# Attention followed by a two-layer MLP: scores in groups of three chunks between whole groups of MLP products, and two shared PSUM banks

## The chip, the core and the metric

The kernel runs on one core of a Trainium2 chip. The metric is the device time of one execution in microseconds (us), and the median over several runs is quoted. Every profile is one execution of its own.

The engines are named as in the profile. PE is TensorE, which multiplies matrices (PEld is its weight load, which overlaps the products). ACT is ScalarE, DVE is VectorE, POOL is GpSimd, and SP is SyncE, which here only issues transfers. SPq is SyncE's queue. PSUM is the memory in which TensorE leaves its results[...].

## The reference

```python
scores = (1.0 / np.sqrt(64)) * np.matmul(q, k.transpose(0, 1, 3, 2))   # q, k, v: (8, 12, 448, 64)
scores = scores - np.max(scores, axis=-1, keepdims=True)
attn = np.exp(scores)
attn = attn / (np.sum(attn, axis=-1, keepdims=True) + 1e-09)
x = np.matmul(attn, v)                                                 # (8, 12, 448, 64)
x = x.transpose(0, 2, 1, 3).reshape(3584, 768)
h = x @ w_in                                                           # (768, 2048)
g = np.maximum(0.01 * h, h)
out = g @ w_out                                                        # (2048, 768), float32
```

The kernel leaves out the subtraction of the maximum. It multiplies in bf16 and accumulates in float32.

## The kernel before

**Units.** A unit `u` is a pair of heads of one batch. There are 8 batches with 6 pairs each, so 48 units (`NU`), and `HP` is 6. For every unit, q, k and v are loaded by SyncE (`load`, L91), cast to bf16 by GpSimd (`cast`, L104), and q and k are turned so that the head dimension lies on partitions (`qkT`). The first 12 units (`NPE`) are turned by TensorE into PSUM (`transposes`, L164) and copied out by VectorE (L173). Later units are turned by a transposing transfer on SyncE's queue (`dma_transposes`, L160).

**Scores.** A unit has four chunks of 112 keys. `scores(u, c)` (L177) makes two products, one for each head of the pair. Each uses 64 rows of the array and has 448 columns. The two results lie in the two banks of one score slot (pool `ps_s`). `expo(u, c)` (L189) lets ScalarE take the exponential of both at once (L191) and write `e`, which frees the slot.

**pv.** `pv(u, j)` (L193) makes 16 small products for one head of the pair, each with 65 columns, the last of which is the sum of the exponentials. VectorE takes the reciprocal (L207) and multiplies (L208). The result `x` is turned into `xT` by `x_transposes` (L212): through TensorE and a VectorE copy for units below 9, and by a transposing transfer for the later ones.

**MLP.** `mlp(i)` (L236) works on 384 or 512 tokens in turn, four batches of each, the first with 384. It has 16 groups of six products for the first layer (L243, called w_in below), each group evacuated by ScalarE (L248). Then it has 6 or 8 groups of 16 products with 384 columns for the second layer (L260, called w_out below), each evacuated by VectorE (L265). A finished row block of `o` is stored by SyncE (`store`, L225). `mlp` is a generator: it hands back control after every single product.

**Order.** The order is written out by hand, so every engine runs its instructions in the order of the program. `slots(u)` (L306) gives eight steps for a unit: scores of two chunks in step 0, their exponentials in steps 0 and 1, `pv` of the unit before in steps 2 and 6, transposes in steps 1 and 3, the scores of the other two chunks in step 4. The first six units run alone (L362). From then on, 60 steps are spread over the products of MLP batch 0 and 48 steps over each of batches 1 to 6. The steps fall between single products, wherever the count of columns says so (L370 to L376). Batch 7 has no attention beside it.

**PSUM.** There are two score slots of two banks each (`ps_s`), one bank for transposes (`ps_tr`), one bank for pv (`ps_pv`), and two for MLP products (`ps_mm`), L58 to L61. A product that starts a new result in a slot waits for the last reader of the old one.

**Weights.** `load_w` issues eight transfers from GpSimd's queue, one early and seven in units 2 to 5.

Of the kernel before, what the change touches and what calls it, by code (L numbers as in the profile page):

```python
# [16 lines left out]
def kernel(  # L17
# [9 lines left out]
    nc = tc.nc  # L27
# [27 lines left out]
    h_pool = ctx.enter_context(tc.tile_pool(name="h", bufs=2))  # L55
    o_pool = ctx.enter_context(tc.tile_pool(name="o", bufs=3))

    ps_s = ctx.enter_context(tc.tile_pool(name="ps_s", bufs=2, space=PSUM))  # L58
    ps_tr = ctx.enter_context(tc.tile_pool(name="ps_tr", bufs=1, space=PSUM))
    ps_pv = ctx.enter_context(tc.tile_pool(name="ps_pv", bufs=1, space=PSUM))  # L60
    ps_mm = ctx.enter_context(tc.tile_pool(name="ps_mm", bufs=2, space=PSUM))  # L61


    NV = 5
# [67 lines left out]

    def warm_up(n):
        for _ in range(n):
            ps = ps_mm.tile([P, 512], F32, name="mm")
            nc.tensor.matmul(ps, warm[:, :P], warm, start=True, stop=True)  # L136

    warm_up(9)
# [21 lines left out]
    def dma_transposes(u):  # L160
        if NPE <= u < NU:
            turn(qkT[u % NQ][:, :QL], qk_sb[u].rearrange("p i so h d -> p (i so h d)"))

    def transposes(u):  # L164
        if u >= min(NPE, NU):
            return
        tr = ps_tr.tile([P, 2, S], BF16, name="tr")
        for i in range(2):
            for so in range(NSC):
                nc.tensor.transpose(  # L170
                    tr[:, i, ts(so, SC)], qk_sb[u][:, i, so], ident[:SC, :SC]
                )
        nc.vector.tensor_copy(qkT[u % NQ][:, :QL], tr.rearrange("p i s -> p (i s)"))  # L173
# [19 lines left out]
    def pv(u, j):  # L193

        e, vt = e_sb[u % NE], v_sb[u % NV]
        ps = ps_pv.tile([P, NSC, D + 1], F32, name="pv")
        for qc in range(NSC):
            for c in range(NSC):
                at = (j * NSC + c) * S + qc * SC
                nc.tensor.matmul(  # L200
                    ps[:, qc, :], e[:, at:at + P], vt[:, j, c, :],
                    start=(c == 0), stop=(c == NSC - 1),
                )
        if j == 0:
            x_t[u] = x_pool.tile([SC, NSC, 2, D], BF16, name="x")
        rec = r_pool.tile([SC, NSC, 1], F32, name="rec")
        nc.vector.reciprocal(rec, ps[:SC, :, D:])  # L207
        nc.vector.tensor_mul(  # L208
            x_t[u][:, :, j, :], ps[:SC, :, :D], rec.to_broadcast([SC, NSC, D])
        )  # L210

    def x_transposes(u):  # L212
        b, hp = divmod(u, HP)
        at = b * S % NX
        dst = xT[:, hp, at:at + S]
        if u >= NPE - 3:
            turn(dst, x_t.pop(u).rearrange("p so h d -> p (so h d)"))
            return
        tr = ps_tr.tile([P, 2, S], BF16, name="tr")
        for so in range(NSC):  # L220
            nc.tensor.transpose(tr[:, 0, ts(so, SC)], x_t[u][:, so], ident[:SC, :SC])  # L221
        nc.vector.tensor_copy(dst, tr[:, 0, :])  # L222


    def store(o, t0):  # L225

        done = 0
        while done < P:
# [4 lines left out]
            nc.sync.dma_start(out=dst[so, p:p + n], in_=o[done:done + n, :])  # L233
            done += n

    def mlp(i):  # L236
        n = cuts[i + 1] - cuts[i]
        at = cuts[i] % NX
        h = h_pool.tile([P, MD, 4 * P], BF16, name="h")
        for m in range(MD):  # L240
            ps = ps_mm.tile([P, 4 * P], F32, name="mm")
            for kk in range(KD):
                nc.tensor.matmul(  # L243
                    ps[:, :n], w_in_sb[:, kk, ts(m, P)], xT[:, kk, at:at + n],
                    start=(kk == 0), stop=(kk == KD - 1),
                )
                if kk == KD - 1:
                    nc.scalar.activation(h[:, m, :n], ps[:, :n], AX.Prelu, alpha=0.01)  # L248
                yield n

        todo = [(c, w) for c in range(n // P) for w in range(2)]
        if i == 0:
            todo.sort(key=lambda cw: cw[1])
        o = {}
        for c, w in todo:
            if c not in o:
                o[c] = o_pool.tile([P, DM], F32, name="o")
            ps = ps_mm.tile([P, 4 * P], F32, name="mm")
            for m in range(MD):
                nc.tensor.matmul(  # L260
                    ps[:, :NW], h[:, m, ts(c, P)], w_out_sb[:, m, ts(w, NW)],
                    start=(m == 0), stop=(m == MD - 1),
                )
                if m == MD - 1:
                    nc.vector.tensor_copy(o[c][:, ts(w, NW)], ps[:, :NW])  # L265
                    if w == 1:
                        store(o.pop(c), cuts[i] + c * P)
                yield NW


    def turning_slots(u):


        def s0():
            pv(u - 1, 0)
            x_transposes(u - 2)

        def s1():
            pv(u - 1, 1)
            transposes(u)  # L280

        def s2():
            x_transposes(u - 1)

        def s3():
            scores(u, 0)
            scores(u, 1)
            expo(u, 0)
            load(u + 5)

        def s4():
            expo(u, 1)
            transposes(u + 1)

        def s5():
            scores(u, 2)
            scores(u, 3)
            expo(u, 2)
            cast(u + 3)

        def s6():
            expo(u, 3)

        return [s0, s1, s2, s3, s4, s5, s6, lambda: None]

    def slots(u):  # L306

        on = u < NU

        def s0():  # L310
            if on:
                scores(u, 0)
                scores(u, 1)
                expo(u, 0)
            if u == 0:
                warm_up(4)

        def s1():
            if on:
                expo(u, 1)  # L320
            if 2 <= u <= NU + 1 and u - 2 not in (HP - 2, HP - 1):
                x_transposes(u - 2)
            dma_transposes(u + 2)

        def s2():
            if 1 <= u <= NU:
                pv(u - 1, 0)

        def s3():
            load(u + 5)  # L330
            load_w({2: 1, 3: 2, 4: 2, 5: 2}.get(u, 0))
            if u + 1 < NU and u + 1 != HP:
                transposes(u + 1)

        def s4():
            if on:
                scores(u, 2)
                scores(u, 3)
                expo(u, 2)

        def s5():
            if on:
                expo(u, 3)
            cast(u + 3)

        def s6():
            if 1 <= u <= NU:
                pv(u - 1, 1)

        def s7():  # L350
            pass

        return [s0, s1, s2, s3, s4, s5, s6, s7]

    steps = [s for u in range(NU + 2) for s in (turning_slots if u == HP else slots)(u)]

    begin = [8 * (HP * (i + 1) + 1) + 7 for i in range(B)]
    begin[0] = 8 * HP + 3
    assert begin[B - 1] == 8 * (NU + 1) + 7
    transposes(0)  # L360
    warm_up(2)
    for s in steps[:begin[0]]:  # L362
        s()
    for i in range(B):
        work = steps[begin[i]:begin[i + 1]] if i + 1 < B else []
        n = cuts[i + 1] - cuts[i]
        total = MD * KD * n + n // P * MD * DM
        used = 0
        atoms = mlp(i)
        for j, s in enumerate(work):  # L370
            s()
            while used < total * (j + 1) // len(work):
                step = next(atoms, None)
                if step is None:
                    break
                used += step  # L376
        for _ in atoms:
            pass


# [28 lines left out]
```

## Time and profile before

| | us |
|---|---|
| median of 7 runs | 427.86 |
| lowest and highest run | 426.55 and 429.44 |
| time of the profiled execution | 428.95 |
| its span, first to last instruction | 427.2 |

| group of the profile | count | busy, us | mean of one, ns |
|---|---|---|---|
| L191 exponential, ACT | 192 | 167.9 | 915 |
| L243 w_in products, PE | 768 | 163.3 | 355 |
| L260 w_out products, PE | 896 | 160.7 | 326 |
| L200 pv products, PE | 1536 | 65.1 | 194 |
| L182 score products, PE | 384 | 54.7 | 357 |
| L248 first-layer evacuation, ACT | 128 | 69.8 | 545 |
| L265 second-layer evacuation, DVE | 56 | 31.2 | 557 |
| L208 and L207 after pv, DVE | 96 each | 40.7 and 17.5 | 424 and 182 |

How to read it: products on TensorE are pipelined, so the mean duration of one is longer than its share of the engine. The distance between two starts is what a product costs. The busy time of a group is the time in which at least one of its instructions ran.

TensorE's clock is granted in full except in the stretch from 30 to 40 us, where the mean is 0.66. The 16 transfer engines are saturated over the first 80 us (207 to 287 GB/s in stretches of 10 us), since the weights come in beside q, k and v.

### The profile page before, as it was taken

Reading aid. Unit: us, or ns where it says so; the run is one execution under the profiler, and the core shown is the slowest. Engines: PE = TensorE matmul, PEld = TensorE weight load, DVE = VectorE, ACT = ScalarE, POOL = GpSimd, SP = SyncE. Lnnn points to the kernel's source line nnn. Section 1 sums busy time; section 2 is a strip of 40 time slices with the busy share of each in tenths; the row PEclk is TensorE's granted clock in tenths of the full one; section 3 lists DMA queues with packets and bytes.
Section 4 is the critical chain, followed back from the end, with each engine's and each line's share of the span. In section 5 each row is a group of like instructions: output and inputs, shape, how many; then the busy total and the mean of one; then the engine's idle time right before and its main releaser. Section 6 shows DMA issues by size and latency. Waiting matters only on the chain.

```text
span 427.2 us, 8997 instructions
## 1 busy us (share of the span) xinstructions
PE 414.1 (97%) x3731; PEld 226.9 (53%) x3731; DVE 100.2 (23%) x271; ACT 229.8 (54%) x322; POOL 92.1 (22%) x168
## 2 busy tenths in 40 slices
PE   7879999999999999999999999999999999999995
PEld 2554665544555555544455555554455555654563
DVE  1542333221132212221122212221123211320021
ACT  4866775567634676457643476456753477314300
POOL 4494332331111222211311131221112100000000
PEclk9997999999999999999999999999999999999999
DMA  8999999984555966675374977686445440230022
GB/s 207 255 245 246 249 250 215 267 221 109 111 143 160 209 130 167 180 184 137 97 146 126 185 181 136 183 193 153 128 99 142 112 90 13 59 85 2 0 75 74
DMA packets 98505, 63.66 MB, mean 149 GB/s; under 512 B 55456, under 2 KB 94880, under 8 KB 98464
## 3 DMA queue, kind: packets, MB, share of 16 engines
q1 hardware_dynamic: 90928, 56.56, 55.5%
q0 software_dynamic: 7296, 6.29, 9.2%
q8 instruction: 29, 0.48, 0.5%
q10 hardware_dynamic: 240, 0.23, 0.2%
q14 instruction: 12, 0.10, 0.1%
HBM read 45.61 MB, written 11.01 MB: 133 GB/s over the span
## 4 chain that ended last, share of the span: by engine, by line
PE 94%; ACT 2%; DMA 1%; issue 1%; POOL 1%; DVE 1%; SPq 0%; ACTq 0%
PE mm L243 35%; PE mm L260 35%; PE pv L200 11%; PE sc L182 10%; ACT e L191 2%; PE tr L170 1%; DMA fv<-in_v_dram 1%; PE tr L221 0%; POOL w_in_sb L124 0%; DVE x L208 0%; DVE qkT L173 0%; POOL qkb L109 0%; POOL v L111 0%; POOL qkb L110 0%; DVE o L265 0%
## 5 line engine op out<-in xcount | busy, mean ns | idle before, releaser
L191 ACT ACTIVATE e<-sc 112x896 bf16<-112x896 f32 x192 | 167.9, 915 | 109.6 <-PE sc L182 109.4
L243 PE MATMUL mm<-xT,w_in_sb 128*128 128x384 bf16 (+1 forms) x768 | 163.3, 355 | 0.0
L260 PE MATMUL mm<-w_out_sb,h 128*128 128x384 bf16 x896 | 160.7, 326 | 0.0
L260 PEld LDWEIGHTS <-h 128*128 128x128 bf16 x896 | 81.4, 98 | 62.3 <-issue 14.5
L243 PEld LDWEIGHTS <-w_in_sb 128*128 128x128 bf16 x768 | 68.5, 98 | 71.4 <-issue 17.5
L248 ACT ACTIVATE h<-mm 128x384 bf16<-128x384 f32 (+1 forms) x128 | 69.8, 545 | 59.1 <-PE mm L243 59.1
L111 POOL CAST v<-fv 112x512 bf16<-112x512 f32 x48 | 29.6, 617 | 202.8 <-PE pv L200 176.5
L200 PEld LDWEIGHTS <-e 112*128 112x128 bf16 x1536 | 61.2, 98 | 16.1 <-DVE x L208 2.2
L207 DVE RECIPROCAL rec<-pv 112x4 f32<-112x4 f32 x96 | 17.5, 182 | 211.2 <-PE pv L200 210.7
L200 PE MATMUL pv<-v,e 112*128 112x65 bf16 x1536 | 65.1, 194 | 1.4 <-DVE x L208 1.4
L182 PE MATMUL sc<-qkT 64*128 64x448 bf16 x384 | 54.7, 357 | 4.3 <-ACT e L191 3.2
L265 DVE COPY o<-mm 128x384 f32<-128x384 f32 x56 | 31.2, 557 | 86.7 <-PE mm L260 86.5
L208 DVE TENSOR_TENSOR x<-pv,rec 112x256 bf16<-112x256 f32 x96 | 40.7, 424 | 3.5 <-DVE rec L207 0.3
L109 POOL CAST qkb<-fq 112x512 bf16<-112x512 f32 x47 | 28.9, 615 | 34.2 <-DMA fq<-in_q_dram 17.9
L182 PEld LDWEIGHTS <-qkT 64*128 64x128 bf16 x384 | 12.1, 94 | 36.4 <-issue 31.3
L110 POOL CAST qkb<-fk 112x512 bf16<-112x512 f32 x47 | 28.9, 614 | 9.8 <-DMA fk<-in_k_dram 9.4
L173 DVE COPY qkT<-tr 128x896 bf16<-128x896 bf16 x12 | 7.5, 621 | 7.4 <-PE tr L170 7.2
L170 PE MATMUL tr<-ident,qkb 112*128 112x112 bf16 x96 | 8.0, 227 | 0.6 <-ACT qkb L110 0.2
L170 PEld LDWEIGHTS <-qkb 112*128 112x128 bf16 x96 | 6.3, 106 | 3.0 <-DVE qkb L109 0.7
L136 PE MATMUL mm<-warm 128*128 128x512 bf16 x15 | 5.1, 488 | 1.2 <-DVE warm L131 1.2
L222 DVE COPY xT<-tr 128x448 bf16<-128x448 bf16 x9 | 3.5, 390 | 9.8 <-PE tr L221 9.8
L221 PE MATMUL tr<-ident,x 112*128 112x112 bf16 x36 | 3.5, 222 | 0.7 <-DVE qkT L173 0.7
(17 smaller groups left out, 15.0 us busy)
## 6 DMA issues: line engine op xcount, KB each, us to landing
fq<-in_q_dram SPq DMA_DIRECT2D x48, 224.0 KB, 3.7
fv<-in_v_dram SPq DMA_DIRECT2D x48, 224.0 KB, 4.2
fk<-in_k_dram SPq DMA_DIRECT2D x47, 224.0 KB, 3.8
w_in_sb<-in_moe_w_in_dram POOLq DMA_DIRECT2D x4, 768.0 KB, 15.3
w_out_sb<-in_moe_w_out_dram POOLq DMA_DIRECT2D x4, 768.0 KB, 34.9
out_dram<-o SPq DMA_DIRECT2D x8, 336.0 KB, 3.0
out_dram<-o SPq DMA_DIRECT2D x8, 288.0 KB, 2.7
out_dram<-o SPq DMA_DIRECT2D x8, 240.0 KB, 3.3
```

Source lines behind the costliest of these rows:

```text
L109: by[0](qk_sb[u][:, 0].rearrange("p so h d -> p h so d"), fq)
L110: by[1](qk_sb[u][:, 1].rearrange("p so h d -> p h so d"), fk)
L111: by[2](v_sb[u % NV][:, :, :, :D], fv)
L170: nc.tensor.transpose(tr[:, i, ts(so, SC)], qk_sb[u][:, i, so], ident[:SC, :SC])
L182: nc.tensor.matmul(ps[:, j, :S], t[j * D:(j + 1) * D, S + c * SC:S + c * SC + P], t[j * D:(j + 1) * D, :S], start=True, stop=True,)
L191: nc.scalar.activation(e[:, :, c, :], sc_t.pop((u, c))[:SC, :, :S], AX.Exp, scale=scale)
L200: nc.tensor.matmul(ps[:, qc, :], e[:, at:at + P], vt[:, j, c, :], start=(c == 0), stop=(c == NSC - 1),)
L208: nc.vector.tensor_mul(x_t[u][:, :, j, :], ps[:SC, :, :D], rec.to_broadcast([SC, NSC, D]))
L243: nc.tensor.matmul(ps[:, :n], w_in_sb[:, kk, ts(m, P)], xT[:, kk, at:at + n], start=(kk == 0), stop=(kk == KD - 1),)
L248: nc.scalar.activation(h[:, m, :n], ps[:, :n], AX.Prelu, alpha=0.01)
L260: nc.tensor.matmul(ps[:, :NW], h[:, m, ts(c, P)], w_out_sb[:, m, ts(w, NW)], start=(m == 0), stop=(m == MD - 1),)
L265: nc.vector.tensor_copy(o[c][:, ts(w, NW)], ps[:, :NW])
```

## The change

**PSUM.** `ps_s` has three score slots instead of two, and a single pool `ps_g` with two banks serves MLP products, transposes and pv in turn.

**MLP.** `mlp` hands back control only between whole groups of products. The evacuation stands right behind the group.

**Attention.** The first six units run through `first(u)`, in the same order as before. From unit 6 on there are clusters instead of slots. Three units are four clusters, and cluster `g` has `t, r = divmod(g, 4)` and `u = 3 * t`. Each cluster makes the scores of three consecutive chunks in one go. Two of the exponentials are issued at once; the third is put on a list, `late`, which `settle()` empties behind the next evacuation of the first layer or ahead of the next group of the second. A cluster with two heads of pv to do (`r` 2 and 3) makes one ahead of its scores and one behind; the others make one behind. Transposes of x come first in a cluster and those of q and k last, where TensorE does them.

**Loads and casts.** Three of four clusters hold a cast and a load, and the transposing transfer of a unit is issued at the end of clusters with `r` above 0, behind that cluster's load.

**Placing.** Clusters 8 to 18 go into MLP batch 0, the first of them ahead of it, and eight clusters into each of batches 1 to 6. A cluster runs when the columns done so far have reached its share. With 384 tokens that is, in the first layer, after every fourth group (in batch 0 after groups 4, 7, 10, 13 and 16). The last cluster of a batch stands at its end.

```diff
-    ps_s = ctx.enter_context(tc.tile_pool(name="ps_s", bufs=2, space=PSUM))
-    ps_tr = ctx.enter_context(tc.tile_pool(name="ps_tr", bufs=1, space=PSUM))
-    ps_pv = ctx.enter_context(tc.tile_pool(name="ps_pv", bufs=1, space=PSUM))
-    ps_mm = ctx.enter_context(tc.tile_pool(name="ps_mm", bufs=2, space=PSUM))
+    ps_s = ctx.enter_context(tc.tile_pool(name="ps_s", bufs=3, space=PSUM))
+    ps_g = ctx.enter_context(tc.tile_pool(name="ps_g", bufs=2, space=PSUM))
...
-        tr = ps_tr.tile([P, 2, S], BF16, name="tr")
+        tr = ps_g.tile([P, 2, S], BF16, name="tr", tag="g")
...
-        ps = ps_pv.tile([P, NSC, D + 1], F32, name="pv")
+        ps = ps_g.tile([P, NSC, D + 1], F32, name="pv", tag="g")
...
+    late = []
+
+    def settle():
+        while late:
+            expo(*late.pop(0))
+
     def mlp(i):
...
-            ps = ps_mm.tile([P, 4 * P], F32, name="mm")
+            ps = ps_g.tile([P, 4 * P], F32, name="mm", tag="g")
             for kk in range(KD):
                 nc.tensor.matmul(
                     ps[:, :n], w_in_sb[:, kk, ts(m, P)], xT[:, kk, at:at + n],
                     start=(kk == 0), stop=(kk == KD - 1),
                 )
-                if kk == KD - 1:
-                    nc.scalar.activation(h[:, m, :n], ps[:, :n], AX.Prelu, alpha=0.01)
-                yield n
+            nc.scalar.activation(h[:, m, :n], ps[:, :n], AX.Prelu, alpha=0.01)
+            settle()
+            yield KD * n
...
         for c, w in todo:
+            settle()
...
-                if m == MD - 1:
-                    nc.vector.tensor_copy(o[c][:, ts(w, NW)], ps[:, :NW])
-                    if w == 1:
-                        store(o.pop(c), cuts[i] + c * P)
-                yield NW
+            nc.vector.tensor_copy(o[c][:, ts(w, NW)], ps[:, :NW])
+            if w == 1:
+                store(o.pop(c), cuts[i] + c * P)
+            yield MD * NW
...
+    def first(u):
+
+        scores(u, 0)
+        scores(u, 1)
+        expo(u, 0)
+        if u == 0:
+            warm_up(4)
+        expo(u, 1)
+        if u >= 2:
+            x_transposes(u - 2)
+        if u >= 1:
             pv(u - 1, 0)
+        load(u + 5)
+        load_w({2: 1, 3: 2, 4: 2, 5: 2}.get(u, 0))
+        if u + 1 < HP:
+            transposes(u + 1)
+        scores(u, 2)
+        scores(u, 3)
+        expo(u, 2)
+        expo(u, 3)
+        cast(u + 3)
+        if u >= 1:
             pv(u - 1, 1)
...
+    def cluster(g):
+        t, r = divmod(g, 4)
+        u = 3 * t
+        chunks = [divmod(4 * u + 3 * r + x, NSC) for x in range(3)]
+        chunks = [(a, c) for a, c in chunks if a < NU]
+        heads = [[(u - 1, 0)], [(u - 1, 1)], [(u, 0), (u, 1)], [(u + 1, 0), (u + 1, 1)]][r]
+        heads = [(a, j) for a, j in heads if HP <= a < NU]
+        turned = {0: u - 2, 2: u - 1, 3: u}.get(r)
+        if turned is not None and HP <= turned < NPE - 3:
+            x_transposes(turned)
+        if len(heads) > 1:
+            pv(*heads.pop(0))
+        for a, c in chunks:
+            scores(a, c)
+        for a, c in chunks[:2]:
+            expo(a, c)
+        late.extend(chunks[2:])
+        for a, j in heads:
+            pv(a, j)
+            if j == 1 and a >= NPE - 3:
+                x_transposes(a)
+        if r < 3:
+            cast(u + 3 + r)
+            load(u + 5 + r)
+        transposes({3: u + 3, 0: u + 1, 1: u + 2}.get(r, NU))
+        if r > 0:
+            dma_transposes(u + 2 + r)
...
     transposes(0)
     warm_up(2)
-    for s in steps[:begin[0]]:
-        s()
+    for u in range(HP):
+        first(u)
+    u = HP - 1
+    pv(u, 0)
+    x_transposes(u - 1)
+    pv(u, 1)
+    transposes(HP)
+    x_transposes(u)
+
+
+    begin = [8 * (i + 1) + 3 for i in range(B)]
+    begin[0] = 8
     for i in range(B):
-        work = steps[begin[i]:begin[i + 1]] if i + 1 < B else []
+        work = list(range(begin[i], begin[i + 1])) if i + 1 < B else []
         n = cuts[i + 1] - cuts[i]
         total = MD * KD * n + n // P * MD * DM
-        used = 0
-        atoms = mlp(i)
-        for j, s in enumerate(work):
-            s()
-            while used < total * (j + 1) // len(work):
-                step = next(atoms, None)
-                if step is None:
-                    break
-                used += step
-        for _ in atoms:
-            pass
+        used, done = 0, 0
+        lead = 1 if i == 0 else 0
+
+        def catch_up():
+            nonlocal done
+            while done < len(work) and used * (len(work) - lead) >= total * (done + 1 - lead):
+                settle()
+                cluster(work[done])
+                done += 1
+
+        catch_up()
+        for step in mlp(i):
+            used += step
+            catch_up()
```

## The prediction

> **What bounds the kernel now.** I read the page first (busy shares, slices, chain), then the waits of TensorE, then the timeline of a quiet stretch, then the tail of the chain, then the transposing transfers.
>
> ```profile
> PE 414.1 (97%) x3731; PEld 226.9 (53%) x3731; DVE 100.2 (23%) x271; ACT 229.8 (54%) x322; POOL 92.1 (22%) x168
> ...
> PE mm L243 35%; PE mm L260 35%; PE pv L200 11%; PE sc L182 10%; ACT e L191 2%; PE tr L170 1%; DMA fv<-in_v_dram 1%; PE tr L221 0%; POOL w_in_sb L124 0%; DVE x L208 0%; DVE qkT L173 0%; POOL qkb L109 0%; POOL v L111 0%; POOL qkb L110 0%; DVE o L265 0%
> ```
>
> The chain is TensorE nearly throughout. The largest of its nine waits (us in total, times, longest):
>
> ```profile
> PE sc L182 <- ACT e L191: 3.2, 7, 0.8
> PE pv L200 <- DVE x L208: 1.4, 2, 0.8
> PE mm L136 <- DVE warm L131: 1.2, 1, 1.2
> PE tr L221 <- DVE qkT L173: 0.7, 1, 0.7
> ```
>
> All nine sum to 7.9 us and, by the timeline, lie before 34 us, where the first MLP product runs. After that TensorE never waits for data. So a gain must come from TensorE's own rate. The last batch has no attention beside it, and the chain gives the clean rates:
>
> ```profile
> 380.65 20.72 PE mm L243 x96
> 401.37 20.81 PE mm L260 x128
> ```
>
> That is 0.216 us for a product of 512 columns and 0.163 us for one of 384. Against these, the timeline inside the first full batch:
>
> ```profile
> 89.84 1.89 PE L243 MATMUL mm<-xT,w_in_sb 128*128 128x512 bf16 x8
> ...
> 91.66 0.55 PE L182 MATMUL sc<-qkT 64*128 64x448 bf16 x4
> ...
> 92.13 0.92 ACT L191 ACTIVATE e<-sc 112x896 bf16<-112x896 f32 x1 [0.19 <-PE sc L182]
> ...
> 92.15 1.90 PE L243 MATMUL mm<-xT,w_in_sb 128*128 128x512 bf16 x8
> ...
> 93.88 0.68 PE L200 MATMUL pv<-v,e 112*128 112x65 bf16 x16
> ...
> 94.40 1.89 PE L243 MATMUL mm<-xT,w_in_sb 128*128 128x512 bf16 x8
> 94.60 0.18 DVE L207 RECIPROCAL rec<-pv 112x4 f32<-112x4 f32 x1 [3.92 <-PE pv L200]
> ...
> 94.82 0.42 DVE L208 TENSOR_TENSOR x<-pv,rec 112x256 bf16<-112x256 f32 x1
> ```
>
> Take differences of start times. Eight products cost 92.15 to 93.88 = 1.73 us before a pv, but 89.84 to 91.66 = 1.82 us before a score burst: 0.09 us lost on entering. Sixteen pv products cost 0.52 us and lose nothing. The score burst holds its place for 91.66 to 92.15 = 0.49 us. One score product lasts 0.36 us (row L182) and the burst 0.55, so the second pair starts 0.19 us after the first; the two heads of a pair overlap. Two pairs cost 0.39 us at that rate; the other 0.10 is lost on leaving. Each burst loses 0.19 us.
>
> **What the Trainium skill says.** *TensorEngine Tiling (Array Packing)*, Tiling Modes, Key Properties: changing the tiling mode drains TensorE. The trace agrees: 0.09 us in and 0.10 us out around 64-row scores, nothing around 112-row pv products. *PSUM — Partial Sum Buffer*, on bank collisions: an engine may not read a bank that TensorE writes, so a slot is free only after its last reader. *Perfetto Trace Analysis*, Optimizing Tensor Performance: product groups should rotate through banks so that evacuation lies beside the next group. Before, transposes, pv and MLP products have one, one and two banks; no wait after 34 us shows that this suffices.
>
> **The change part by part.**
>
> *Fewer bursts.* Units 0 to 5 keep two bursts each. Units 6 to 47 made 84 bursts of two chunks; now 168 chunks go in 56 bursts of three. 28 bursts less at 0.19 us: -5.3 us. The trace has no third pair in a burst; nearest is the second, 0.19 us. Below that it cannot go (384 columns take 0.163, so 448 take 0.19). At worst it is the 0.29 us from the last pair to the next product, then 56 x 0.10 = 5.6 us are given back. I take 0.19.
>
> *Start.* A third score slot removes the waits for L191, but in units 2 to 4 the casts wait for transfers, and from 24.39 to 29.46 us the exponentials already run without a gap; no gain there. At 32.6 us the transpose of unit 5 waited for the single transpose bank (the 0.7 us above); with two banks it does not, and the next scores wait only for the copy of qkT, which ends at 33.30, instead of starting at 33.82: -0.45 us.
>
> *Two banks for everything else, steady part.* A pv bank is free when L208 ends: 94.82 + 0.42 = 95.24, 0.84 us after the pv; with 0.06 us to restart TensorE, 0.90. A w_in bank: 0.20 us until L248 starts, 0.49 us for it (384 columns, L248's group), 0.06: 0.75. A w_out bank: 0.20 + 0.56 (L265) + 0.06 = 0.82. Products alternate, so a bank is asked for again after one other product. Whole groups of 0.98, 1.30 or 2.60 us cover all of these. The tight case is ScalarE's order for 384 columns: two exponentials at once, the third behind the next L248. Counted from the start of a cluster: first pair at 0.09, exponentials from 0.09 + 0.47 = 0.56 (0.47 is 91.66 to 92.13), 0.81 us apart back to back, ScalarE free at 2.18. TensorE: burst 0.09 + 0.68 = 0.77, pv to 1.29, group 1 to 2.27. L248 of group 1 at 2.47, ScalarE free 2.85 (0.38 later), third exponential to 3.65, L248 of group 2 to 4.15, bank free 4.21. Group 4 wants it at 1.29 + 3 x 0.98 = 4.22. It fits by 0.01 us. With 512 columns the margin is over 0.4 us. Batches 2, 4 and 6 have 12 such clusters; between 0 and 0.1 us each, 0 to 1.2: I take +0.3.
>
> *Two banks, first batch.* Here transposes still go through PSUM, and they are shorter than an evacuation:
>
> ```profile
> 61.70 0.36 PE L221 MATMUL tr<-ident,x 112*128 112x112 bf16 x4
> ...
> 61.89 0.82 PE L260 MATMUL mm<-w_out_sb,h 128*128 128x384 bf16 x4
> ...
> 63.55 0.56 PE L170 MATMUL tr<-ident,qkb 112*128 112x112 bf16 x8
> ...
> 63.94 0.65 PE L260 MATMUL mm<-w_out_sb,h 128*128 128x384 bf16 x3
> ```
>
> Four x transposes hold TensorE 0.19 us, eight qk transposes 0.39. Cluster 11 runs x transposes, then pv in the bank of the group just ended: 0.75 - 0.19 = 0.56 us of wait. After pv and qk transposes the next group wants the pv bank: 0.90 - 0.39 = 0.51, in clusters 11, 12 and 13. Cluster 14 repeats the first case behind a w_out group: 0.82 - 0.19 = 0.63. Sum +2.7 us, queued behind it all of TensorE. Cluster 8 has no pv, 9 has none either, 10 no transposes: no wait. Bounds 0 and 4.
>
> *Moved transfers.* Cluster 13 puts the load of unit 15 ahead of the transposing transfer of unit 12 on SyncE's queue; before it stood behind. The queue is full there:
>
> ```profile
> DMA to landing us min/median/max: 2.3/2.9/15.8
> ...
> 55.53 6.04 SPq L158 DMA_TRANSPOSE qkT<-qkb  x1
> ...
> 60.00:64.00 4.00, 4.00 (x48) 2.52 (x47) 1.45 (x5) 2.73 (x5) 1.12 (x2) 1.00 1.21 250
> ```
>
> That transfer is the slowest one, landing at 71.35. Three loads of 224 KB at a spacing of about 1.7 us (SyncE's loads between 50.0 and 53.3) push it 5 us, to 76.4. Its first scores, cluster 16, come at my count at 78. Unit 13's transfer follows x's on the same queue and lands near 82 to 83, where cluster 17 asks at 82. I take +0.5, bounds 0 and 5. Later clusters have three clusters (some 15 us) of lead against 3 us of transfer. GpSimd's casts move with the loads; none waits for more than a pv of its own cluster.
>
> *Last batch.* The last pv stands one w_out group before it. x is ready 0.52 + 0.84 = 1.36 us after that pv starts, lands 2.3 to 2.7 us later, at most 4.1; wanted at 0.52 + 2.60 + 5 x 0.216 = 4.2 us (the sixth product of the first group). Nothing, by 0.1 us.
>
> Sum: -5.3 - 0.45 + 0.3 + 2.7 + 0.5 = -2.25 us. The profiled execution took 428.95 us (span 427.2 and 1.75 around it), giving 426.7. It lies 1.09 above the median of the runs, 427.86, which gives **425.6 us**.
>
> **The rivals.** *A, likeliest:* as summed. *B, waits vanish:* the bank waits of the first batch fall into time that the transfers cost anyway and the tight margins hold. For it: transfers there set the pace of the casts. Against: nothing after 34 us waits now. -5.3 - 0.45 = -5.75, so 422.1. *C, the gain is eaten by ScalarE's order:* the 0.01 us margin fails, 0.2 us in each of 12 clusters, 2.4 in place of 0.3: 427.7, no change. *D, slower:* unit 12's transposing transfer is late at cluster 16 and units 13 and 14 behind it; TensorE, in order, stands still there. At 15.8 us from an issue near 60 plus what the weights still hold back, a landing at 84 instead of 76.4 costs 84 - 78 = 6 us in place of 0.5: 425.6 + 5.5 = 431.1. It decides the sign once the landing passes about 82. Against: the weight loads end near 74 and the queue empties.
>
> **How the numbers follow.** A 0.47, B 0.20, C 0.18, D 0.15. A's own range is 423.8 to 427.2; the whole is 421.8 to 429.8, reaching into B and the near side of D. A measurement tells 0.3%, 1.3 us, from no change. Faster takes B and most of A (0.64); same takes C and A's upper edge (0.20); slower is D and a bad C (0.16).
>
> **What would show it.** Right: 384 score products in 68 bursts, TensorE losing 0.19 us at each; small TensorE waits for L208 and L248 between 48 and 70 us, summing near 2.7; none in the batches of 512. Wrong: third pairs at 0.29; TensorE waiting for qkT transfers at 78 to 87 us; L243 waiting for L248 once per cluster in batches 2, 4 and 6; or last-batch products waiting for the x transfer.

## The result, and the profile after

| | before | after |
|---|---|---|
| median, us (runs) | 428.11 (31) | 424.70 (12) |
| lowest and highest, us | 426.51 to 432.37 | 422.36 to 426.81 |
| profiled execution, us | 428.95 | 425.59 |
| its span, us | 427.2 | 423.8 |

The ratio of after to before is 0.9909, with an interval of 0.9885 to 0.9933: 0.9% or 3.9 us faster, between 2.9 and 4.9 us. This is the difference of the means; the medians differ by 3.4 us. Ratios leave out executions more than 1.5% above the fastest of their kernel (three of 20 in one experiment below), medians are over all. The forecast was 425.6.

The page of after: span, busy shares, and the chain that ended last.

```profile
span 423.8 us, 9000 instructions
...
PE 408.8 (96%) x3731; PEld 234.3 (55%) x3731; DVE 99.7 (24%) x271; ACT 228.3 (54%) x322; POOL 91.1 (21%) x168
...
PE mm L250 34%; PE mm L268 34%; PE pv L199 12%; PE sc L181 9%; DMA fv<-in_v_dram 3%; DMA fq<-in_q_dram 1%; DMA xT<-x 1%; DVE x L207 1%; DVE o L272 1%; SPq L97 1%; ACT e L190 0%; PE tr L169 0%; DVE rec L206 0%; POOL qkb L108 0%; POOL v L110 0%
```

The same 3731 products keep TensorE busy 5.3 us less. L181 is now the score line, L190 its exponential, L199 pv, L207 the multiplication behind it, L250 and L254 the first layer and its evacuation, L268 and L272 the second. In the chain the transfer of `xT` is new, and L207 and L272 have 1% each, where their lines had 0% before. TensorE's waits after 42 us in after (us in total, times, longest), where before had none at all:

```profile
PE mm L250 <- DMA xT<-x: 1.6, 1, 1.6
PE mm L250 <- DVE x L207: 0.7, 2, 0.3
PE pv L199 <- DVE o L272: 0.5, 1, 0.5
PE pv L199 <- ACT h L254: 0.4, 1, 0.4
PE mm L268 <- DVE x L207: 0.3, 1, 0.3
```

The timeline of TensorE in after, batch 0 (start, duration, then the wait ahead of it in brackets):

```profile
48.10 0.67 PE L199 MATMUL pv<-v,e 112*128 112x65 bf16 x16 [0.38 <-ACT h L254]
48.70 0.74 PE L181 MATMUL sc<-qkT 64*128 64x448 bf16 x6
49.38 0.69 PE L199 MATMUL pv<-v,e 112*128 112x65 bf16 x16
49.90 0.56 PE L169 MATMUL tr<-ident,qkb 112*128 112x112 bf16 x8
50.80 3.10 PE L250 MATMUL mm<-xT,w_in_sb 128*128 128x384 bf16 x18 [0.34 <-DVE x L207]
...
66.46 0.36 PE L220 MATMUL tr<-ident,x 112*128 112x112 bf16 x4
67.27 0.67 PE L199 MATMUL pv<-v,e 112*128 112x65 bf16 x16 [0.45 <-DVE o L272]
...
85.66 1.24 PE L250 MATMUL mm<-xT,w_in_sb 128*128 128x512 bf16 x5
...
88.52 1.67 PE L250 MATMUL mm<-xT,w_in_sb 128*128 128x512 bf16 x7 [1.61 <-DMA xT<-x]
```

Three things are to be seen. A burst of six score products holds its place for 49.38 - 48.70 = 0.68 us; one of four held 0.49, so the third pair costs 0.19. After the eight transposes of 49.90 the next group begins 0.90 us later, where the transposes themselves take 0.39: 0.51 us lost for the pv bank. (The view shows 0.34, since the end of a product is modelled and reaches past its slot. Distances between starts are used from here on.) And batch 1, the first with 512 columns, begins at 85.66 and stands still after five products, waiting for `xT`.

In before, the timeline shows the same point, the first product with 512 columns, here:

```profile
86.15 1.03 PE L243 MATMUL mm<-xT,w_in_sb 128*128 128x512 bf16 x4
```

This point cuts every trace into two stretches that behave differently. In the table the stretch up to it holds the start, where the transfers are saturated, and batch 0. The rest, less the one wait for `xT` in it, hardly differs between executions of one kernel: TensorE's clock is granted in full there, in every trace but one.

| trace | first product of batch 1, us | wait for xT, us | rest of the span without it, us |
|---|---|---|---|
| before | 86.15 | 0 | 341.03 |
| before, second profile | 88.46 | 0 | 341.03 |
| after | 85.66 | 1.78 | 336.37 |
| after, second profile | 86.84 | 1.74 | 336.37 |

From batch 1 on the change saves 4.66 us. Up to it the two profiled executions differ by 0.49 us, and the new wait takes 1.78 back: -4.66 - 0.49 + 1.78 = -3.37, the difference of the spans.

### The profile page after: what moved, and what is told of

Same layout as the page of the kernel before. It is cut to its first block, busy times and chain, and to the rows that moved or that the text cites. A ratio compares the mean times of both kernels' runs of the same rounds, so it can differ in the third digit from the quotient of the medians.

```text
span 423.8 us, 9000 instructions
## 1 busy us (share of the span) xinstructions
PE 408.8 (96%) x3731; PEld 234.3 (55%) x3731; DVE 99.7 (24%) x271; ACT 228.3 (54%) x322; POOL 91.1 (21%) x168
## 4 chain that ended last, share of the span: by engine, by line
PE 90%; DMA 5%; DVE 2%; ACT 1%; SPq 1%; POOL 0%; issue 0%; ACTq 0%
PE mm L250 34%; PE mm L268 34%; PE pv L199 12%; PE sc L181 9%; DMA fv<-in_v_dram 3%; DMA fq<-in_q_dram 1%; DMA xT<-x 1%; DVE x L207 1%; DVE o L272 1%; SPq L97 1%; ACT e L190 0%; PE tr L169 0%; DVE rec L206 0%; POOL qkb L108 0%; POOL v L110 0%
## 5 line engine op out<-in xcount | busy, mean ns | idle before, releaser
L190 ACT ACTIVATE e<-sc 112x896 bf16<-112x896 f32 x192 | 164.4, 917 | 104.1 <-PE sc L181 103.9
L250 PE MATMUL mm<-xT,w_in_sb 128*128 128x384 bf16 (+1 forms) x768 | 150.9, 353 | 2.3 <-DMA xT<-x 1.6
L268 PE MATMUL mm<-w_out_sb,h 128*128 128x384 bf16 x896 | 150.5, 326 | 0.6 <-DVE x L207 0.3
L268 PEld LDWEIGHTS <-h 128*128 128x128 bf16 x896 | 85.8, 98 | 55.4 <-DVE x L207 0.5
L250 PEld LDWEIGHTS <-w_in_sb 128*128 128x128 bf16 x768 | 73.2, 98 | 68.5 <-issue 2.6
L254 ACT ACTIVATE h<-mm 128x384 bf16<-128x384 f32 (+1 forms) x128 | 69.6, 544 | 62.6 <-PE mm L250 62.5
L199 PEld LDWEIGHTS <-e 112*128 112x128 bf16 x1536 | 56.8, 98 | 29.8 <-issue 18.5
L199 PE MATMUL pv<-v,e 112*128 112x65 bf16 x1536 | 66.0, 194 | 2.8 <-ACT e L190 1.4
L272 DVE COPY o<-mm 128x384 f32<-128x384 f32 x56 | 31.2, 557 | 133.7 <-PE mm L268 133.7
L181 PE MATMUL sc<-qkT 64*128 64x448 bf16 x384 | 49.6, 356 | 0.7 <-DVE qkT L172 0.2
L207 DVE TENSOR_TENSOR x<-pv,rec 112x256 bf16<-112x256 f32 x96 | 40.7, 424 | 3.3
L181 PEld LDWEIGHTS <-qkT 64*128 64x128 bf16 x384 | 13.8, 94 | 19.9 <-issue 10.5
```

Of the source, the lines that this page charges most:

```text
L181: nc.tensor.matmul(ps[:, j, :S], t[j * D:(j + 1) * D, S + c * SC:S + c * SC + P], t[j * D:(j + 1) * D, :S], start=True, stop=True,)
L190: nc.scalar.activation(e[:, :, c, :], sc_t.pop((u, c))[:SC, :, :S], AX.Exp, scale=scale)
L199: nc.tensor.matmul(ps[:, qc, :], e[:, at:at + P], vt[:, j, c, :], start=(c == 0), stop=(c == NSC - 1),)
L207: nc.vector.tensor_mul(x_t[u][:, :, j, :], ps[:SC, :, :D], rec.to_broadcast([SC, NSC, D]))
L250: nc.tensor.matmul(ps[:, :n], w_in_sb[:, kk, ts(m, P)], xT[:, kk, at:at + n], start=(kk == 0), stop=(kk == KD - 1),)
L268: nc.tensor.matmul(ps[:, :NW], h[:, m, ts(c, P)], w_out_sb[:, m, ts(w, NW)], start=(m == 0), stop=(m == MD - 1),)
```

## The experiments

In the diffs `+` and `-` are relative to the kernel after, unless it says otherwise.

**One burst made two.** Is a burst really 0.19 us? The third chunk's scores go behind the pv, so that each cluster switches twice.

```diff
-        for a, c in chunks:
+        for a, c in chunks[:2]:
             scores(a, c)
...
         transposes({3: u + 3, 0: u + 1, 1: u + 2}.get(r, NU))
+        for a, c in chunks[2:]:
+            scores(a, c)
```

> The changed kernel, with the third score chunk of every cluster issued behind the cluster's pv and transposes, so that each cluster has two score bursts in place of one. Theory 1 (each burst costs 0.19 us of drain, whatever else the change does): 56 more bursts, 56 x 0.19 = 10.6 us, less some 1.4 us, since the late burst of 0.47 us covers three of the waits for a shared bank in batch 0 (0.50 us each). So +9.2 us on the changed kernel's 424.7: about 434. Theory 2 (the gain comes from the start and the clock, and the drain is hardly saved because a longer burst pays it per pair): at most +3 us, below 428.

Measured: median 436.10 us of 4 runs, ratio 1.0186 (1.0146 to 1.0226), 11.4 us above after. The timeline of TensorE in one cluster:

```profile
100.54 0.55 PE L181 MATMUL sc<-qkT 64*128 64x448 bf16 x4
101.02 0.68 PE L199 MATMUL pv<-v,e 112*128 112x65 bf16 x16
101.63 0.36 PE L181 MATMUL sc<-qkT 64*128 64x448 bf16 x2
101.93 5.35 PE L250 MATMUL mm<-xT,w_in_sb 128*128 128x512 bf16 x24
```

The lone pair holds TensorE for 0.30 us, where a third pair inside a burst costs 0.19, and the pv ahead of it lasts 0.61 instead of 0.52: 0.11 and 0.09 us, leaving and entering. The rest of the span (from batch 1 on, as in the table) is 345.86 us, 9.49 more than in after, over 45 bursts: 0.21 each. The products are the same; only the number of switches differs.

**All three exponentials at once.** Is the list `late` what keeps ScalarE off the path?

```diff
-        for a, c in chunks[:2]:
+        for a, c in chunks:
             expo(a, c)
-        late.extend(chunks[2:])
```

> The changed kernel, with all three exponentials of a cluster issued at once, ahead of the next evacuation by ScalarE. Theory 1 (the order that was walked through in the forecast, with a margin of 0.01 us for 384 columns, is the true one): ScalarE is free 0.56 + 3 x 0.81 = 2.99 us after the start of a cluster, the first evacuation ends at 3.48, its bank is free at 3.54, and group 3 wants it at 3.24: 0.30 us of wait in each of the 12 first-layer clusters of batches 2, 4 and 6, and 0 to 0.3 in four of batch 0; none with 512 columns. +3.6 to +4.8 us on 424.7: about 429. Theory 2 (ScalarE has slack enough, the order of its exponentials decides nothing): 424.7.

Measured: 429.65 us, median of 20 runs, ratio 1.0027 (1.0006 to 1.0048), 5.0 us above after. The rest of the span is 339.82 us, 3.45 more than in after. The timeline of TensorE between two clusters in a batch of 384 columns, with all three at once:

```profile
143.98 4.34 PE L250 MATMUL mm<-xT,w_in_sb 128*128 128x384 bf16 x24
148.26 0.74 PE L181 MATMUL sc<-qkT 64*128 64x448 bf16 x6
```

and in after:

```profile
147.05 4.06 PE L250 MATMUL mm<-xT,w_in_sb 128*128 128x384 bf16 x24
151.05 0.74 PE L181 MATMUL sc<-qkT 64*128 64x448 bf16 x6
```

The 24 products of after cost 24 times 0.1625 = 3.90 us up to the burst's entry, as the next pv shows where a pv follows (141.34 to 145.24); with three exponentials ahead of the evacuation they take 0.28 more. Twelve such clusters, 0.27 to 0.30 us each, make up the 3.45. The other 1.5 us of the 5.0 can't be read here: the profiled execution took 425.73 us, the fastest of the 20. From batch 1 on the order of ScalarE matters only with 384 columns, and there the margin that was worked out as 0.01 us held.

**Transposes elsewhere in the cluster.** The bank waits come from transposes that follow a pv. Here q and k are turned ahead of the scores and x behind them, so that a burst of 0.68 us, which needs no shared bank, lies between.

```diff
-        if turned is not None and HP <= turned < NPE - 3:
-            x_transposes(turned)
         if len(heads) > 1:
             pv(*heads.pop(0))
+        transposes({3: u + 3, 0: u + 1, 1: u + 2}.get(r, NU))
         for a, c in chunks:
             scores(a, c)
...
         late.extend(chunks[2:])
+        if turned is not None and HP <= turned < NPE - 3:
+            x_transposes(turned)
...
-        transposes({3: u + 3, 0: u + 1, 1: u + 2}.get(r, NU))
```

> The changed kernel, with the q and k transposes of a cluster ahead of its scores and the x transposes behind them, so that the score burst (0.77 us) lies between a short product and the next request for its bank. Theory 1 (five waits for a bank in batch 0, 2.64 us in the profile of the changed kernel, come from the two shared banks): four small ones remain, 0.36 + 0.13 + 0.13 + 0.13 = 0.75 us, so -1.9 us: about 422.8. Theory 2 (what these waits cost is waited for anyway, at the x transfer ahead of batch 1): the profile shows the bank waits gone and the wait of the first w_in group of batch 1 longer by as much; 424.7.

Measured: 424.68 us, median of 20 runs, ratio 0.9903 (0.9879 to 0.9926): the time of after. The profiled execution took 427.98 us and has 3.4 us of half clock early in batch 1, so only the place of its waits is read. The longest:

```profile
PE mm L250 <- DMA xT<-x: 2.0, 1, 2.0
PE mm L268 <- DMA w_out_sb<-in_moe_w_out_dram: 2.0, 2, 1.3
```

The bank waits of L207, L254 and L272 are gone from batch 0, but for 0.23 and 0.13 us, and TensorE stands still instead where the second layer's weights land. In before and after their four parts land at 54.2, 61.1, 68.1 and 74.1 to 74.3 us; here the two waits end with the landings at 61.9 and 75.1. What is saved ahead of such a point is waited for at it. The second profile of after, which reached the second layer 0.8 us earlier than the first and whose weights landed 1.0 to 1.6 us later, shows the same beside its unchanged bank waits:

```profile
PE mm L268 <- DMA w_out_sb<-in_moe_w_out_dram: 1.7, 2, 1.1
```

The bank waits measure 0.54, 0.50, 0.50, 0.50 and 0.61 us in both profiles of after.

> The changed kernel, unchanged: a second profile. Theory 1 (the wait for the x transfer of unit 11 in batch 1 comes and goes with the load on the transfer engines, the five bank waits of batch 0 do not): the bank waits are 0.54, 0.50, 0.50, 0.50 and 0.61 us again, within 0.05; the x wait may be anything from 0 to 2.2 us. Theory 2 (both are fixed): the x wait is 1.8 us again.

It took 426.72 us.

**One load later.** What is the wait for `xT`? The timeline of SyncE's queue in after (start, duration of the issue):

```profile
79.88 0.71 SPq L97 DMA_DIRECT2D fq<-in_q_dram  x1
80.63 0.49 SPq L97 DMA_DIRECT2D fk<-in_k_dram  x1
81.17 0.46 SPq L97 DMA_DIRECT2D fv<-in_v_dram  x1
81.72 0.87 SPq L232 DMA_DIRECT2D out_dram<-o  x2
82.69 2.18 SPq L157 DMA_TRANSPOSE xT<-x  x1
```

The transposing transfer of unit 11's x is issued behind the three loads of unit 17 and two stores, and lands at 88.48, 5.8 us after its issue. That order is not new. In before the queue holds the same loads and stores ahead of the same transfer:

```profile
78.18 0.57 SPq L98 DMA_DIRECT2D fq<-in_q_dram  x1
...
79.86 0.88 SPq L233 DMA_DIRECT2D out_dram<-o  x2
80.84 1.40 SPq L158 DMA_TRANSPOSE xT<-x  x1
```

There it was issued 5.3 us before batch 1 began (80.84 and 86.15) and landed after 3.8. In after it is issued 3.0 us before (82.69 and 85.66), because the last pv of unit 11 starts 4.9 us ahead of batch 1 instead of 7.3. Would it land in time without the load ahead? Here the load goes into the next cluster, behind that transfer.

```diff
-            load(u + 5 + r)
+            if g == 17:
+                load(17)
+            if g != 16:
+                load(u + 5 + r)
```

> The changed kernel, with the load of unit 17 moved from cluster 16 to cluster 17, behind the transposing transfer of x of unit 11. Theory 1 (that transfer took 5.8 us to land because a load and two stores lay ahead of it): it lands some 2 us earlier, and the wait of 1.78 us in the first w_in group of batch 1 goes: about 423. Theory 2 (the transfer is held up by the stores, or starts late because of the pv before it): the wait stays, 424.7.

Measured: 423.23 us, median of 5 runs, ratio 0.9916 (0.9877 to 0.9956); by the time it can't be told from after. In its trace nothing waits for `xT`, and one wait is new:

```profile
PE mm L268 <- DMA w_out_sb<-in_moe_w_out_dram: 0.6, 1, 0.6
```

Its batch 1 begins at 84.87 and its rest is 336.35 us. The transfer landed 2.7 us after its issue. Over all traces it took 3.6 to 6.0 us in the eleven with the load ahead, and 2.7 to 2.9 in the three with the load behind, so the load does delay it. But the load alone makes no wait: in two kernels with after's order on the queue (three exponentials at once, and one burst made two) it took 4.3 and 3.6 us, was issued 3.5 and 4.1 us before batch 1, and nothing waited. The wait takes both, the late issue and the load.

**Both together.** Transposes as above, and the loads of units 15, 16 and 17 a cluster later (unit 18's stays in its cluster).

```diff
-            load(u + 5 + r)
+        for a in {13: [], 14: [15], 15: [16], 16: [], 17: [17, 18]}.get(g, [u + 5 + r] if r < 3 else []):
+            load(a)
```

> The changed kernel with the reordered transposes (q and k ahead of the scores, x behind) and with the loads of units 15 to 18 one cluster later, behind the transposing transfers of x. Theory 1 (in the reordered kernel the time came back as waits for the second-layer weights near 62 and 75 us and for the x transfer of unit 11, because the loads compete with them for the transfer engines): the weights' last part lands about 2 us before 74 us, and both gains show, -1.9 for the banks and -1.8 for x: about 421. Theory 2 (the weights land no earlier, since the loads were not what held them up): 423 at best.

Measured: 422.55 us, median of 6 runs, ratio 0.9866 (0.9829 to 0.9902). Of TensorE's waits none for a bank, the weights or `xT` is listed after 42 us, its batch 1 begins at 86.18 after 10.2 us at half clock, and its rest is 336.36. The largest wait that is left lies in the start:

```profile
PE tr L169 <- POOL qkb L109: 1.7, 2, 1.5
```

One edit alone gained nothing that can be measured. The median with both lies 2.1 us below after's, though the intervals just overlap, and 0.7 us below that with one load moved, which is within the noise.

**The new start alone.** The kernel before with three score slots and two shared banks in the first six units only, and its own pools afterwards.

```diff
-    ps_s = ctx.enter_context(tc.tile_pool(name="ps_s", bufs=2, space=PSUM))
-    ps_tr = ctx.enter_context(tc.tile_pool(name="ps_tr", bufs=1, space=PSUM))
...
+    start = ExitStack()
+    ps_s = start.enter_context(tc.tile_pool(name="ps_s0", bufs=3, space=PSUM))
+    ps_tr = ps_pv = ps_mm = start.enter_context(tc.tile_pool(name="ps_g0", bufs=2, space=PSUM))
```

> The kernel before, with three score slots and two shared banks in its first six units alone; from unit 6 on it has its own four pools again. Theory 1 (the third score slot brings the start forward: in the profile of the changed kernel the first scores of unit 6 come 1.7 us earlier, and the half-rate stretch of the clock is 3.4 us in place of 6.8): -2 to -3.5 us on 428.1, about 425.5. Theory 2 (the start is bound by transfers, as forecast, and the shorter half-rate stretch is an accident of one profile): -0.5 us, 427.6.

Measured: 427.75 us, median of 20 runs, ratio 0.9985 (0.9966 to 1.0004): -0.6 us, and no change is not excluded. A second profile of it:

> The kernel of e4_before_new_start, unchanged: a second profile of its start. Theory 1 (the wait of 2.2 us for a cast at 20 us in its first profile was chance): the first scores of unit 6 come near 32 us, as in the changed kernel. Theory 2: they come near 34 us, and the third slot does nothing for the start.

It took 427.09 us, with its first scores of unit 6 at 31.78 us, 2 us ahead of before. Its waits show where that went:

```profile
PE mm L259 <- DMA w_out_sb<-in_moe_w_out_dram: 1.8, 2, 1.2
```

**The old start under the new rest.** The kernel after with the four pools of before until unit 5 is done.

```diff
+    start = ExitStack()
+    ps_s = start.enter_context(tc.tile_pool(name="ps_s0", bufs=2, space=PSUM))
+    ps_tr = start.enter_context(tc.tile_pool(name="ps_tr0", bufs=1, space=PSUM))
+    ps_pv = start.enter_context(tc.tile_pool(name="ps_pv0", bufs=1, space=PSUM))
+    ps_g = start.enter_context(tc.tile_pool(name="ps_mm0", bufs=2, space=PSUM))
...
+    start.close()
+    ps_s = ctx.enter_context(tc.tile_pool(name="ps_s", bufs=3, space=PSUM))
+    ps_tr = ps_pv = ps_g = ctx.enter_context(tc.tile_pool(name="ps_g", bufs=2, space=PSUM))
```

> The changed kernel, with the PSUM pools of the kernel before (two score slots, one bank for transposes, one for pv) in its first six units alone. Theory 1 (the new start is worth what the kernel before gained from it, 0.7 us by the means): 425.3. Theory 2 (it is worth the 2.5 us by which the two first profiles differ at 42 us, and carries most of the change's gain): 427.

Measured: 426.51 us, median of 22 runs, ratio 0.9969 (0.9951 to 0.9987), 1.8 us above after's median. Of its waits two count here:

```profile
PE sc L184 <- ACT e L193: 3.2, 7, 0.8
...
PE sc L184 <- DVE xT L224: 0.5, 1, 0.5
```

The first is before's wait for a score slot, to the digit. The second belongs to the change of pools: the first scores of unit 6 wait 0.5 us until the old pools are empty, and that much is the price of the experiment. By the ratios to their own runs of before, the two kernels lie 2.6 us apart rather than 1.8. Its batch 1 begins at 88.53, after `xT` has landed, and waits for nothing there.

**Idle products at the start.** In the profiles the granted clock near 32 us differs. This is the windows view of before (window, then busy time and count of each engine, then PEclk):

```profile
32.00:34.00 2.00, 1.29 (x13) 0.93 (x13) 1.24 (x4) 0.00 (x0) 1.92 (x3) 0.50 1.18 246
34.00:36.00 2.00, 2.00 (x9) 0.65 (x6) 0.32 (x1) 1.52 (x2) 0.62 (x1) 0.50 1.19 246
36.00:38.00 2.00, 2.00 (x14) 1.12 (x14) 0.62 (x1) 0.64 (x2) 0.61 (x1) 0.50 1.18 247
```

and of after:

```profile
32.00:34.00 2.00, 1.93 (x15) 0.92 (x15) 0.47 (x2) 1.21 (x2) 1.46 (x3) 0.50 1.18 247
34.00:36.00 2.00, 2.00 (x13) 1.17 (x11) 0.62 (x1) 0.72 (x2) 0.62 (x1) 0.71 1.18 245
36.00:38.00 2.00, 2.00 (x14) 1.19 (x13) 0.00 (x0) 1.73 (x4) 0.61 (x1) 1.00 1.17 243
```

TensorE ran at half rate for 6.8 us in before and 3.4 in after. Is that the change's doing? A kernel with eight products whose result nobody reads, put where TensorE waits between 27 and 32 us, should tell.

```diff
+    fill = ps_s.tile([P, 2, 512], F32, name="sc")
+
+    def filler(n):
+        for _ in range(n):
+            nc.tensor.matmul(fill[:, 0, :], warm[:, :P], warm, start=True, stop=True)
+
+    filler(5)
     pv(u, 0)
+    filler(2)
...
+    filler(1)
```

> The changed kernel, with eight products of 512 columns on zeros, whose result nobody reads, put into TensorE's waits between the last pv of unit 4 and the first scores of unit 6 (27 to 32 us). Theory 1 (the half-rate stretch that begins near 31 us in most profiles is set off by these waits): it is gone in the profile, and 1 to 3 us with it: about 423. Theory 2 (it depends on something else): the stretch stays, 424.7.

Measured: 424.84 us, median of 8 runs, ratio 0.9916 (0.9886 to 0.9946): the time of after. In the profile the half rate is gone, and batch 1 begins at 84.00, 1.7 us ahead of after. But the weights then took 0.65 us and `xT` 1.92. A second profile of before was taken beside it:

> The kernel before, unchanged: a second profile of its start. Theory 1 (the start of the changed kernel is earlier by the third score slot): the first scores of unit 6 come near 33.8 us again, against 32.0 in three profiles of the changed start. Theory 2 (chance): they come at 32 to 33 us.

It took 431.29 us, with 10.2 us at half rate in two stretches, from 23.5 and from 33.7 us. So one kernel differs from execution to execution by as much as the two kernels did, and the shorter stretch in after can't be put down to the change.

**All three.** The transposes, the loads and the idle products in one kernel.

> The kernel of e8_reorder_loads with the eight filling products of e6_filler. Theory 1 (the filler removes the half-rate stretch near 31 us; in e6_filler that gain was spent on waiting for the second-layer weights and for x, and here the loads are out of their way): about 421, 1.5 us below e8_reorder_loads. Theory 2 (batch 0 is held to the pace of the transfers whatever TensorE does): the profile shows the wait for w_out near 73 us again, and 422.5.

Measured: 421.39 us, median of 6 runs (419.97 to 422.86), ratio 0.9856 (0.9820 to 0.9892), the fastest kernel of the study, though not to be told from the one without idle products. Batch 1 begins at 82.78 us, the rest is 336.37. Nothing waits for the weights or for `xT`.

## Why the prediction was right, and where it was off

The direction came from the right cause, and the forecast lay 0.9 us above the median. The sum was -2.25 us; the runs say -3.9 (2.9 to 4.9), or -3.4 by the medians, so it was too small by 0.7 to 2.7 us.

*Fewer bursts, 28 at 0.19 us, -5.3.* Right. Third pairs cost 0.19 us and no more. From batch 1 on the bursts fall from 68 to 45, which at 0.19 is -4.4; with the +0.3 of the steady part, -4.1 were forecast for that stretch, and -4.66 measured. Summed over distances of starts, the 68 bursts lose 12.96 us in before, 0.19 each, and the 45 lose 8.11 in after, 0.18 each: -4.85. One pair of scores less in this stretch and small amounts around the pv make -0.4, and two waits at the end of batch 6, below, +0.6. Splitting the burst gave 0.21 per burst the other way. *TensorEngine Tiling (Array Packing)*, Tiling Modes, says that a change of mode drains TensorE; these traces agree as far as they show it, a loss on both sides of a burst of 64 rows.

*Two banks in the first batch, +2.7.* The waits came where they were put, 0.54, 0.50, 0.50, 0.50 and 0.61 us in clusters 11 to 14, 2.6 in all, against 2.7. (The 0.06 us to restart TensorE in that sum stands in no line shown; the waits of before end 0.03 to 0.05 us ahead of the next product, once 0.14.) That this is also what they cost in the end is not shown: with the waits gone (transposes elsewhere) the time stayed, and TensorE waited for the weights and for `xT` instead. With the loads moved too the median falls by 2.1 us, but the wait for `xT`, 1.8 us, goes with the loads. So what the two banks cost stays open, between nothing and the 2.6 us of their waits. In this, rival B's mechanism, waits that fall into time which the transfers cost, was at least in part true; its 422.1 is not what came.

*Two banks, steady part, +0.3.* In the 12 clusters with 384 columns, for which it stood, it measured nothing: no evacuation of ScalarE was waited for. Rival C's 0.2 us per cluster is what comes, at 0.28, if the third exponential is not held back. Missed were the two clusters at the end of batch 6 that have pv but no scores left: each pv there is shorter than the evacuation that the next group waits for, 0.29 us each, +0.6. *PSUM — Partial Sum Buffer*, on bank collisions, says that two engines must not be on one bank at the same time; the waits of this case agree, since each ends with the last reader of the bank.

*Moved transfers, +0.5, for the qkT of units 12 and 13.* These two landed at 74.7 and 79.6 us (76.4 and 82 to 83 were forecast), in time. Late was a transfer that the term does not name, that of x of unit 11: 1.78 us in the first group of batch 1. No moved load came ahead of it; its pv moved closer to batch 1. How long before its use the x of a last unit is issued was worked out for the last batch alone, with 2.3 to 4.1 us to land. At batch 1 the transfer had 4.1 us (82.69 to 86.74, where the sixth product would have started) and took 5.8. A late transposing transfer is what rival D feared, but it was another one, for another reason, and cost a third of D's 5.5 us.

*Start, -0.45.* This term was too small. The end of unit 5's exponentials and the first scores of unit 6 in before:

```profile
24.39 5.07 ACT L191 ACTIVATE e<-sc 112x896 bf16<-112x896 f32 x6 [0.71 <-PE sc L182]
...
33.82 0.93 PE L182 MATMUL sc<-qkT 64*128 64x448 bf16 x4
```

and in after,

```profile
23.86 4.95 ACT L190 ACTIVATE e<-sc 112x896 bf16<-112x896 f32 x6 [1.00 <-PE sc L181]
...
32.13 1.30 PE L181 MATMUL sc<-qkT 64*128 64x448 bf16 x6
```

with a wait of TensorE that is new there (us in total, times, longest):

```profile
PE pv L199 <- ACT e L190: 1.4, 3, 0.6
```

The exponentials end at 29.46 and 28.81, 0.65 us earlier, where "no gain there" was said of the third score slot. From their end to the scores it is 4.36 and 3.32 us, 1.0 less where 0.45 was forecast; some of this may be the clock, which was halved from 31.3 us on in before and from 31.7 in after. The reason given was not wrong: the 3.2 us of waits for L191 vanish, and with the old start they come back, but 1.4 us of them return as pv waiting for exponentials, so ScalarE does bind there. What the start is worth in the end is 0.6 us by the one experiment, which might be none, and up to 1.8 by the medians or 2.6 by the ratios of the other, 0.5 of which is the price of its change of pools. It is no fixed amount: an earlier start ends at the weights, as the 1.8 us in the second profile of the new start show, or at `xT`.

*Last batch, 0.* Right: no wait there.

So the stretch from batch 1 on is settled to a few tenths of a microsecond. Up to it the forecast was +1.8 us with the transfers (-0.45 for the start, -0.95 for five bursts less, +2.7 and +0.5), and the two profiled executions show -0.49 + 1.78 = +1.3 in its place, with 3.4 us less of half rate in after, while the runs at large say +0.8 by the means (-3.9 + 4.66) and +1.3 by the medians. How this rest divides between the start, the waits hidden by the weights and the clock stays open: it differs between executions of one kernel by 2.3 us in before (86.15 and 88.46) and 1.2 in after. That the sum came this close is partly luck: the wait for `xT` cost 1.3 us more than the term for transfers had, and the first scores of unit 6 came 1.2 us earlier than the term for the start had, which offset each other.

## What to carry to other kernels

Count how often the array changes between tile shapes, and price one burst from the distances of starts; grouping is worth that price times the changes saved, and the saving is kept where nothing but TensorE bounds. When pools are merged, compare each short product with the evacuation that the next user of the bank waits for, and put something long that needs no such bank between them. In a stretch paced by transfers, a wait removed can come back at the next landing, so its length is not yet what it costs. And where work moves towards the end of a stretch, work out for each transfer that depends on it how long before its first use it is issued, and how long it takes behind what stands ahead of it on its queue.

## What the runs showed of the hardware

The half-rate stretches were not expected to differ between executions of one kernel. In the 14 traces TensorE's clock was at half for 0, 3.4, 6.8 or 10.2 us between 19 and 41 us, in steps of 3.4: the two traces of before had 6.8 and 10.2 us, those of the kernel with only the new start 10.2 and none; two more without idle products had none either. *TensorE: Matmul & The Clock Gate*, Part 1: The HAM clock gate, says that the clock follows TensorE's activity over windows of 3413 ns that run freely of the kernel. The steps agree with it, and a free window would explain why the same waits lower the clock in one execution and not in the next; no run here tests that. The page speaks of an idle window; here TensorE was never idle for so long, the longest single wait near a stretch being 2.0 us, and in the windows from 30 to 32 us it was busy for 1.46 and 1.47 of 2 us in before and after. Idle products went with a full clock both times that they were tried, which is too few to call it their doing.

A transposing transfer of x has a median of 2.5 us from issue to landing in after. That of unit 11 took 3.6 to 6.0 us behind three loads of 224 KB and two stores, in eleven traces, and 2.7 to 2.9 us behind stores alone, in three. In a kernel whose TensorE is 96% busy, that one transfer was the longest wait after the start.
